# Outputs of the last batch in staging tiles, and a second queue for the last stores

## The chip, the cores and the metric

The kernel runs on one core of one Trainium2 chip. Its time is device microseconds. A run gives one time; the times stated are medians over runs. A profile is taken of one execution and shows every instruction of the engines: TensorE (PE, with its weight loads PEld), VectorE (DVE), ScalarE (ACT), GpSimd (POOL) and SyncE (SP). DMAs are issued from an engine's queue and carried by sixteen DMA engines.

## The reference

Inputs are `q`, `k`, `v` of shape (8, 8, 576, 64), that is batch, head, token, head dimension, and four weights. All are float32.

```
def _attn_ref(q, k, v):
    ...
    out_d = sm_attn(q_d, k_d, v_d)           # attention over means of 4 tokens: 144 x 144
    out_up = np.repeat(out_d, factor, axis=2)
    ...
    mask = np.abs(pos[:, None] - pos[None, :]) < factor
    ...
    out_local = np.matmul(attn, v)           # attention within 3 tokens either way
    return (out_up + out_local).astype(np.float32)

def _moe_ref(x, w_theta, w_tok_r, w_tok_i, w_ch):
    theta = x @ w_theta
    cos_t, sin_t = (np.cos(theta), np.sin(theta))
    zr = x * cos_t
    zi = x * sin_t
    yr = np.einsum('ts,bsd->btd', w_tok_r, zr)
    yi = np.einsum('ts,bsd->btd', w_tok_i, zi)
    y = yr + yi
    u = x + y
    return (u + np.maximum(u @ w_ch, 0.0)).astype(np.float32)
```

The attention's output, with its heads side by side, is `x` of shape (8, 576, 512), and `_moe_ref` of it is the result.

## The kernel before, in words

The work is cut by batch, eight in all. For each batch the attention is computed in blocks, `x` is kept transposed (channels on the partitions) in `xT`, the angles go through sine and cosine on ACT, their products with `x` go into `z`, and the mixing over tokens (`mx`, L636) is the largest part of TensorE's work. Its result plus `x` is `uT`, also transposed.

The last stage, which the change touches, works on `uT` of one batch in chunks of 128 tokens. A batch has 576 tokens: four chunks, numbered 0 to 3, and 64 tokens that are left, the last tokens. These are handled for two batches at a time. Chunk c of batch b is written (b,c) here.

- `du` (L645) transposes `uT` back, token by token, into `ur` with a transposing DMA, one for each 128 channels. It is issued by SP.
- `ch` (L666) is `u @ w_ch` of a chunk, four matmuls into one PSUM bank. For (7,3) it is done in two halves of 256 channels.
- `rl` (L671, in `out_part`) has DVE take the maximum with zero, add `ur`, and write the float32 result to an output tile. `rm` does so for the second half of (7,3).
- `st` (L675, in `out_store`) stores the tile; `su` the second half of (7,3).
- `ut` (L656) copies the last tokens of two batches together, `dt` (L690) transposes them into `utr`, `ht` (L695) is their matmul, `rt` (L699) their result, and `ss` and `sr` (L704) store it, the even batch's 64 partitions and the odd one's.

The output tiles before are five buffers, `osb`, which chunks and last tokens use in turn; a buffer is written again only when its store has landed. Another set, `stg`, holds sixteen slots of 576 float32 on 128 partitions; inputs and some transposes land there. All DMAs of the kernel are issued by SP, whose queue works in order.

The order on every engine is the order of one list of words, `ORDER`, which is written out by hand. A word names a kind of step in its first two letters, and what follows is the PSUM bank, the slot, or the engine. Steps of one kind are taken in the order of batch and chunk. Each instruction is bound behind the one before it on its engine, so that no engine does its instructions in another order. The end of the list, from the matmul for (6,0):

```
ch7 ch6 ss ch5 rl rl ch7 ch6 ch4 ch3 ch2 du du st uta dt rl rl rl rl st
st st st st rl rl st st rm ht7 rt su ss sr k0
```

Here `ch7` is (6,0), the second `ch7` is (6,3), `ch6` (7,0), `ch4` (7,1), `ch3` (7,2) and `ch2` (7,3); the first `st` is (6,0), and the `ss` in the first line belongs to batches 4 and 5.

Of the kernel before, what the change touches and what calls it, by code (L numbers as in the profile page):

```python
# [14 lines left out]
P = 128  # L15
B = 8
# [3 lines left out]
DM = 512  # L20
# [19 lines left out]
HALF = 64  # L40
# [51 lines left out]
nm nd23 xn nd01 st mx6 th7 mx2 cs xn xd3 mx0 ua ua xcv ua ua xt67 utv ct dx st st xt45 xt23 xa ch1 rl th0 ch6 ch1 ch7  # L92
cs xa xa tt0 zz zz th2 th3 cs st du du ch4 rl zz zz ztg ct dz rl mx2 mx0 mx1 cs ua ua st dxe dx ht0 ua th1 cs th3 dx7
dx zz st st mx2 rl mx1 ua ua cs zz dt mx3 mx1 mx2 zz zz ztg dz mx7 ua mx3 du du du mx6 rt ua ua utg ua st rl du st mx7
mx4 ua ua ua sr mx7 mx6 mx5 ua ua ua du du ua ch7 ch6 ss ch5 rl rl ch7 ch6 ch4 ch3 ch2 du du st uta dt rl rl rl rl st
st st st st rl rl st st rm ht7 rt su ss sr k0
"""


# [1 line left out]
def kernel(  # L101
# [11 lines left out]
    nc = tc.nc  # L113
# [4 lines left out]
    def tiles(n, shape, name, dt=BF16):  # L118
        return [pool.tile(list(shape), dt, name=f"{name}{i}") for i in range(n)]
# [35 lines left out]
    rl = tiles(2, [P, 2, 4], "rl", FP32)  # L155
# [13 lines left out]
    NOSB = 5  # L169
    osb = tiles(NOSB, [P, DM], "osb", FP32)  # L170
# [4 lines left out]
    stg = [stga[:, i, :] for i in range(NSTG)]  # L175
# [17 lines left out]
    def constants():  # L193
# [18 lines left out]
        for n, c in enumerate((0, 1, 4)):  # L212
            cuts = []
            lo = [W0[b] - CH * c for b in (2 * c, 2 * c + 1)]
            st = [STEP * b - W0[b] for b in (2 * c, 2 * c + 1)]
            en = [st[g] + OWN[2 * c + g] for g in range(2)]
            dl, ds, de = lo[1] - lo[0] - W, st[1] - st[0], en[1] - en[0]
            cuts = [(lo[0], 1, dl, -4), (3 - lo[0], -1, -dl, 4)]
            if max(st):
                cuts.append((-st[0], 1, -W - ds, 0))  # L220
            if min(en) < W:
                cuts.append((en[0] - 1, -1, W + de, 0))
            select(full[1 + n], KP, cuts)
# [39 lines left out]
    at = {}  # L263
# [394 lines left out]
    def halves(b, c):  # L658

        return [slice(0, DM // 2), slice(DM // 2, DM)] if (b, c) == (B - 1, 3) else [slice(0, DM)]  # L660

    def ch(b, c, w):
        ps = at["ch", b, c] = bank(w)
        for cols in halves(b, c):
            for dc in range(4):
                nc.tensor.matmul(out=ps[:, cols], lhsT=uT[b % 2][:, dc, P * c:P * c + P], rhs=wch[:, dc, cols],  # L666
                                 start=(dc == 0), stop=(dc == 3))

    def out_part(b, c, cols):
        o = osb[(4 * b + c + b // 2) % NOSB]  # L670
        nc.vector.scalar_tensor_tensor(out=o[:, cols], in0=at["ch", b, c][:, cols], scalar=0.0,  # L671
                                       in1=ur[b % 2][:, c, cols], op0=ALU.max, op1=ALU.add)

    def out_store(b, c, cols):
        nc.sync.dma_start(out=out[b, P * c:P * c + P, cols], in_=osb[(4 * b + c + b // 2) % NOSB][:, cols])  # L675

    def rlf(b, c, w):
        out_part(b, c, halves(b, c)[0])

    def rm(b, c, w):  # L680
        out_part(b, c, halves(b, c)[1])

    def st(b, c, w):
        out_store(b, c, halves(b, c)[0])

    def su(b, c, w):
        out_store(b, c, halves(b, c)[1])

    def dt(i, w):
        nc.sync.dma_start_transpose(out=utr, in_=uts[i % 2].rearrange("p e b t -> p (e b t)"))  # L690
# [4 lines left out]
            nc.tensor.matmul(out=ps, lhsT=uts[i % 2][:, dc, :, :], rhs=wch[:, dc, :], start=(dc == 0), stop=(dc == 3))  # L695

    def rt(i, w):
        o = at["ot", i] = osb[(9 * i + 8) % NOSB]
        nc.vector.scalar_tensor_tensor(out=o, in0=at.pop(("ht", i)), scalar=0.0,  # L699
                                       in1=utr.rearrange("p e d -> p (e d)"), op0=ALU.max, op1=ALU.add)  # L700

    def tail_store(e):
        def step(i, w):
            nc.sync.dma_start(out=out[2 * i + e, 512:576, :], in_=at["ot", i][HALF * e:HALF * e + HALF])  # L704
        return step


# [1 line left out]
    def span(*ns):  # L709
        out = [()]  # L710
        for n in ns:
            out = [x + (i,) for x in out for i in range(n)]
        return out

    STEPS = dict(
        k0=(lambda i, w: None, span(1)), kc=(kc, span(4)), la=(la, span(4)), ca=(ca, span(4)), lb=(lb, span(9)), cb=(cb, span(9)), lc=(lc, span(4)), cc=(cc, span(4)),
# [13 lines left out]
        xm=(xm, [(b, c) for b, c in span(B, 4) if b not in XDMA]), dx=(dx, [(b, c) for b, c in span(B, 4) if b in XDMA]), zz=(zz, span(B, 4)), mx=(mx, span(B, 8)),  # L730
        ua=(ua, span(B, 8)), du=(du, [(b, c) for b, c in span(B, 4) if b not in RPE]), ut=(ut, span(B)), ch=(ch, span(B, 4)), rl=(rlf, span(B, 4)),
        st=(st, span(B, 4)), rm=(rm, [(B - 1, 3)]), su=(su, [(B - 1, 3)]), dt=(dt, span(4)), ht=(ht, span(4)), rt=(rt, span(4)), ss=(tail_store(0), span(4)), sr=(tail_store(1), span(4)),
    )

# [68 lines left out]
```

## Time and profile before

| | |
|---|---|
| median of 3 runs | 233.03 us (232.65 to 233.73) |
| the profiled execution | 233.64 us |
| its span, first to last instruction | 231.9 us |
| TensorE busy | 217.4 us, 94% of the span |
| VectorE busy | 189.0 us, 81% |
| ScalarE busy | 154.0 us, 66% |
| GpSimd busy | 148.0 us, 64% |
| moved by DMA | 49.41 MB, 213 GB/s over the span |
| read from and written to HBM | 33.98 MB and 9.44 MB |
| mean granted clock of TensorE | 0.994 |

Times in rows of the profile are microseconds from the start of the span. A row of a timeline gives the start, the length, the engine, the line, the operation, and the tiles (written, read); in brackets the idle time before it on its engine and what ended it. SPq is SP's queue: a row of it is the time in which SP issues a DMA, not the time of the transfer. A landing is when the transfer's last part has arrived. In the page's slices each digit is a fortieth of the span and shows the busy share in tenths.

### The profile page before, as it was taken

Reading aid. Unit: us, or ns where it says so; the run is one execution under the profiler, and the core shown is the slowest. Engines: PE = TensorE matmul, PEld = TensorE weight load, DVE = VectorE, ACT = ScalarE, POOL = GpSimd, SP = SyncE. Lnnn points to the kernel's source line nnn. Section 1 sums busy time; section 2 is a strip of 40 time slices with the busy share of each in tenths; the row PEclk is TensorE's granted clock in tenths of the full one; section 3 lists DMA queues with packets and bytes.
Section 4 is the critical chain, followed back from the end, with each engine's and each line's share of the span. In section 5 each row is a group of like instructions: output and inputs, shape, how many; then the busy total and the mean of one; then the engine's idle time right before and its main releaser. Section 6 shows DMA issues by size and latency. Waiting matters only on the chain. (4 is left out here: it accounts for less than half of the span.)

```text
span 231.9 us, 9404 instructions
## 1 busy us (share of the span) xinstructions
PE 217.4 (94%) x3943; PEld 152.4 (66%) x3970; DVE 189.0 (81%) x370; ACT 154.0 (66%) x240; POOL 148.0 (64%) x194
## 2 busy tenths in 40 slices
PE   7997799999999999999999999989998999999990
PEld 2475677776878666876776685766655765578640
DVE  6599998999988889889989798797986976576462
ACT  2279999479988899898878997778777034230000
POOL 7679999949997997996967689379912010200000
PEclk9999999999999999999999999999999999999997
DMA  6999889999999899999999976980665375565777
GB/s 203 401 391 357 280 185 256 384 271 171 334 306 156 205 280 313 160 206 254 159 273 330 259 128 173 152 162 10 95 159 91 64 195 130 118 176 156 117 218 244
DMA packets 76795, 49.41 MB, mean 213 GB/s; under 512 B 61136, under 2 KB 61392, under 8 KB 76752
## 3 DMA queue, kind: packets, MB, share of 16 engines
q1 hardware_dynamic: 76752, 48.81, 83.9%
q8 instruction: 31, 0.51, 1.0%
q14 instruction: 12, 0.10, 0.2%
HBM read 33.98 MB, written 9.44 MB: 187 GB/s over the span
## 5 line engine op out<-in xcount | busy, mean ns | idle before, releaser
L636 PE MATMUL PS<-WT,z 128*128 128x288 bf16 x576 | 78.2, 286 | 0.3 <-DVE z L615 0.2
L636 PEld LDWEIGHTS <-z 128*128 128x128 bf16 x576 | 53.9, 98 | 16.5 <-issue 1.3
L641 DVE TENSOR_TENSOR uT<-PS,xT 128x288 bf16<-128x288 f32 x64 | 28.5, 452 | 10.3 <-PE PS L636 9.5
L561 ACT ACTIVATE cs<-PS,pihc 128x512 bf16<-128x512 f32 x32 | 22.1, 689 | 21.2 <-PE PS L556 20.8
L556 PE MATMUL PS<-wth,xT 128*128 128x512 bf16 x116 | 30.6, 379 | 0.9 <-DVE xT L545 0.3
L666 PE MATMUL PS<-wch,uT 128*128 128x512 bf16 (+1 forms) x122 | 29.6, 372 | 1.0 <-issue 0.6
L671 DVE SCALAR_TENSOR_TENSOR osb<-PS,ur 128x512 f32<-128x512 f32 (+1 forms) x33 | 21.9, 670 | 8.9 <-DMA ur<-uT 4.3
L524 DVE TENSOR_TENSOR tmp<-PS,rl 128x512 bf16<-128x512 f32 x40 | 27.7, 691 | 1.4
L490 ACT ACTIVATE pm<-PS 128x1024 bf16<-128x1024 f32 (+1 forms) x24 | 20.5, 880 | 6.6 <-PE PS L482 5.5
L545 DVE TENSOR_TENSOR xT<-PS,xdT 128x928 bf16<-128x928 f32 (+1 forms) x24 | 22.3, 952 | 3.2 <-PE PS L482 1.5
L577 POOL TENSOR_TENSOR zT<-xT,cst 128x512 bf16<-128x512 bf16 x7 | 10.2, 1456 | 22.1 <-ACT cst L574 14.1
L295 POOL CAST k_tm<-st 128x576 bf16<-128x576 f32 x23 | 15.9, 704 | 6.4 <-DMA st<-in_k_dram 6.3
L765 ACT ACT_TABLE_LOAD x15 | 19.2, 1283 | 0.3
L666 PEld LDWEIGHTS <-uT 128*128 128x128 bf16 x132 | 11.9, 98 | 11.2
L329 POOL TENSOR_TENSOR two<-qT 128x576 f32<-128x576 bf16 x14 | 16.5, 1176 | 4.4 <-ACT qT L315 4.2
L562 ACT ACTIVATE cs<-PS 128x512 bf16<-128x512 f32 x32 | 19.1, 597 | 0.0
L295 POOL CAST q_tm<-st 128x576 bf16<-128x576 f32 x24 | 16.8, 715 | 2.1 <-DMA st<-in_q_dram 2.0
L556 PEld LDWEIGHTS <-xT 128*128 128x128 bf16 x128 | 11.4, 98 | 10.3 <-DVE xT L545 0.7
L503 POOL TENSOR_TENSOR pm<-pm,band 128x512 bf16<-128x512 bf16 x16 | 18.1, 1151 | 0.0
L396 POOL CAST v_w<-st 128x512 bf16<-128x512 f32 x21 | 13.0, 642 | 7.6 <-DVE osb L671 7.6
L620 DVE TENSOR_TENSOR z<-PS,cs 128x1024 bf16<-128x1024 bf16 x24 | 15.8, 684 | 1.0 <-issue 0.5
L329 POOL TENSOR_TENSOR two<-kT 128x580 f32<-128x580 bf16 x13 | 15.0, 1151 | 1.5 <-ACT kT L315 0.9
(121 smaller groups left out, 419.3 us busy)
## 6 DMA issues: line engine op xcount, KB each, us to landing
st<-in_k_dram SPq DMA_DIRECT2D x32, 288.0 KB, 6.0
st<-in_q_dram SPq DMA_DIRECT2D x32, 288.0 KB, 6.0
st<-in_v_dram SPq DMA_DIRECT2D x70, 128.0 KB, 5.4
out_dram<-osb SPq DMA_DIRECT2D x31, 256.0 KB, 3.6
out_dram<-osb SPq DMA_DIRECT2D x10, 128.0 KB, 2.8
st<-in_v_dram SPq DMA_DIRECT2D x4, 288.0 KB, 3.7
st<-in_moe_w_tok_r_dram SPq DMA_DIRECT2D x4, 288.0 KB, 4.3
st<-in_moe_w_tok_i_dram SPq DMA_DIRECT2D x4, 288.0 KB, 5.8
```

The costliest lines, as they stand in the source:

```text
L295: COPY[w](out=to, in_=of)
L329: nc.gpsimd.tensor_tensor(out=t, in0=src[:, :, 0:2], in1=src[:, :, 2:4], op=ALU.add)
L490: nc.scalar.activation(out=pm[(3 * b + u) % NPM][:, :, 0:n].rearrange("p e c j w -> p e (c j w)"), in_=at.pop(("ps", b, u))[:, :, 0:4 * W ...
L524: nc.vector.tensor_tensor(out=tmp[(NCH * b + c) % NTMP].rearrange("p g (j d) -> p g j d", d=D), in0=ps[:, :, :, 0:D], in1=r.unsqueeze(3).t ...
L545: nc.vector.tensor_tensor(out=xT[b % 2][:, :, lo:lo + cnt].rearrange("p e (m j) -> p e m j", j=4), in0=at.pop(("xt", b, u))[:, :, 0:cnt].r ...
L556: nc.tensor.matmul(out=ps, lhsT=xT[b % 2][:, dc, P * c:P * c + P], rhs=wth[:, dc, :], start=(dc == 0), stop=(dc == 3))
L561: nc.scalar.activation(out=t[:, 0, :], in_=ps, func=AF.Sin, bias=pihc, scale=1.0)
L636: nc.tensor.matmul(out=ps, lhsT=z[b % 2][:, j, P * dc:P * dc + P], rhs=WT[:, j, cols], start=(j == 0), stop=(j == 8))
L641: nc.vector.tensor_tensor(out=uT[b % 2][:, dc, cols], in0=at.pop(("mx", b, i)), in1=xT[b % 2][:, dc, cols], op=ALU.add)
L666: nc.tensor.matmul(out=ps[:, cols], lhsT=uT[b % 2][:, dc, P * c:P * c + P], rhs=wch[:, dc, cols], start=(dc == 0), stop=(dc == 3))
L671: nc.vector.scalar_tensor_tensor(out=o[:, cols], in0=at["ch", b, c][:, cols], scalar=0.0, in1=ur[b % 2][:, c, cols], op0=ALU.max, op1=ALU.add)
L765: nc.scalar.activation(out=idle, in_=pihc, func=TABLE[kind])
```

## The change

Three things change, all at the end of the kernel.

- The four chunks of batch 7 and the last tokens of batches 6 and 7 are written to slots 0 to 3 and 4 of `stg` in place of `osb`.
- Of the last eleven stores, five are issued by ACT's queue (`a` behind the word): (6,1), (6,3), (7,1), the last tokens of batch 6, and the first half of (7,3). The other six stay with SP.
- The last tokens' matmul, result and stores (`ht7`, `rt`, `ss`, `sr`) stand ahead of those of chunk (7,3), which comes last. The stores alternate with the results that they store.

```
-mx4 ua ua ua sr mx7 mx6 mx5 ua ua ua du du ua ch7 ch6 ss ch5 rl rl ch7 ch6 ch4 ch3 ch2 du du st uta dt rl rl rl rl st
-st st st st rl rl st st rm ht7 rt su ss sr k0
+mx4 ua ua ua sr mx7 mx6 mx5 ua ua ua du du ua ch7 ch6 ss ch5 rl rl ch7 ch6 ch4 ch3 du du st uta dt sta rl st rl ht7
+ch2 sta rl st rl sta rl st rt ssa sr rl sta rm su k0
...
+    def obuf(b, c):
+        return stg[c][:, 0:DM] if b == B - 1 else osb[(4 * b + c + b // 2) % NOSB]
+
     def out_part(b, c, cols):
-        o = osb[(4 * b + c + b // 2) % NOSB]
+        o = obuf(b, c)
...
-    def out_store(b, c, cols):
-        nc.sync.dma_start(out=out[b, P * c:P * c + P, cols], in_=osb[(4 * b + c + b // 2) % NOSB][:, cols])
+    QUEUE = dict(a=nc.scalar)
+
+    def out_store(b, c, cols, w):
+        QUEUE.get(w, nc.sync).dma_start(out=out[b, P * c:P * c + P, cols], in_=obuf(b, c)[:, cols])
...
     def st(b, c, w):
-        out_store(b, c, halves(b, c)[0])
+        out_store(b, c, halves(b, c)[0], w)
...
     def su(b, c, w):
-        out_store(b, c, halves(b, c)[1])
+        out_store(b, c, halves(b, c)[1], w)
...
     def rt(i, w):
-        o = at["ot", i] = osb[(9 * i + 8) % NOSB]
+        o = at["ot", i] = stg[4][:, 0:DM] if i == B // 2 - 1 else osb[(9 * i + 8) % NOSB]
...
     def tail_store(e):
         def step(i, w):
-            nc.sync.dma_start(out=out[2 * i + e, 512:576, :], in_=at["ot", i][HALF * e:HALF * e + HALF])
+            QUEUE.get(w, nc.sync).dma_start(out=out[2 * i + e, 512:576, :], in_=at["ot", i][HALF * e:HALF * e + HALF])
         return step
```

## The prediction

> **What bounds it now.** I read the slices of the page first, to see where the kernel stops being a TensorE kernel, then the chain that ended last, then the timelines of the last fifteen microseconds by engine, and last the DMA load in stretches.
>
> ```profile
> span 231.9 us, 9404 instructions
> ...
> PE   7997799999999999999999999989998999999990
> ...
> ACT  2279999479988899898878997778777034230000
> ...
> DMA  6999889999999899999999976980665375565777
> ```
>
> One slice is 5.8 us. TensorE is full up to the last slice and empty in it; ACT is empty in the last four. So all before 218 us is a TensorE matter that the edit does not touch, and the edit lives in the last slices. The profiled execution took 233.64 us beside its span of 231.9 (1.7 us lie around the span) and is 0.61 us above the median of the runs, 233.03. I work out a difference against the span and take it off both.
>
> ```profile
> 218.59 4.06 PE PS L666 x18
> ...
> 222.68 0.59 DVE osb L671
> 223.27 2.29 DMA out_dram<-osb
> ...
> 225.68 0.61 DVE osb L671
> ...
> 226.34 0.77 DVE osb L671 x2
> ...
> 227.11 0.69 DVE osb L699
> ```
>
> That is the end of the chain (start, length, what). The work of TensorE is on it until 222.66; then DVE's last parts wait for a store: a result can be written only when the store that last used its buffer has landed, 2.29 us after it was issued.
>
> ```profile
> 219.22 0.69 DVE L671 SCALAR_TENSOR_TENSOR osb<-PS,ur 128x512 f32<-128x512 f32 x1 [0.41 <-PE PS L666]
> 220.09 0.69 DVE L671 SCALAR_TENSOR_TENSOR osb<-PS,ur 128x512 f32<-128x512 f32 x1 [0.17 <-PE PS L666]
> ...
> 221.82 0.69 DVE L671 SCALAR_TENSOR_TENSOR osb<-PS,ur 128x512 f32<-128x512 f32 x1 [0.17 <-PE PS L666]
> 222.68 0.69 DVE L671 SCALAR_TENSOR_TENSOR osb<-PS,ur 128x512 f32<-128x512 f32 x1 [0.17 <-PE PS L666]
> 223.94 0.69 DVE L671 SCALAR_TENSOR_TENSOR osb<-PS,ur 128x512 f32<-128x512 f32 x1 [0.57 <-DMA out_dram<-osb]
> 225.68 1.41 DVE L671 SCALAR_TENSOR_TENSOR osb<-PS,ur 128x512 f32<-128x512 f32 x3 [1.05 <-DMA out_dram<-osb]
> 227.11 0.69 DVE L699 SCALAR_TENSOR_TENSOR osb<-PS,utr 128x512 f32<-128x512 f32 x1
> ```
> ```profile
> 225.08 1.03 PE L695 MATMUL PS<-wch,ut 128*128 128x512 bf16 x4
> ```
>
> These are chunks (6,0), (6,1), (6,3), (7,0), (7,1), then (7,2) with the two halves of (7,3), then the last tokens. As long as TensorE sets the pace a chunk comes every 0.86 us (219.22 to 220.09) and takes 0.69. Then come the two waits for a landing, 0.57 and 1.05 us. TensorE itself is through at 225.08 + 1.03 = 226.11.
>
> ```profile
> 218.50 2.53 SPq L645 DMA_TRANSPOSE ur<-uT  x2
> 221.46 0.35 SPq L675 DMA_DIRECT2D out_dram<-osb  x1
> 221.93 1.24 SPq L690 DMA_TRANSPOSE utr<-ut  x1
> 223.27 4.70 SPq L675 DMA_DIRECT2D out_dram<-osb  x8
> 228.06 1.14 SPq L704 DMA_DIRECT2D out_dram<-osb  x2
> ```
> ```profile
> 228.62 0.58 SPq L704 DMA_DIRECT2D out_dram<-osb  x1
> ```
>
> SP's queue (the row by itself is the second of the two before it, from a narrower stretch) shows why the landings are late: (6,1) lay ready at 220.78 and was issued at 223.27, behind two transposes for `ur`, the store of (6,0) and the transpose for `utr`. And at the end four stores still stand in line: DVE ends at 227.80, the last store goes out at 228.62, the span ends 3.31 us after that.
>
> ```profile
> 221.00:225.00 4.00, 4.00 (x24) 2.13 (x23) 2.72 (x4) 0.00 (x0) 0.00 (x0) 1.00 0.68 195
> 225.00:230.00 5.00, 1.10 (x7) 0.36 (x4) 2.10 (x4) 0.00 (x0) 0.00 (x0) 0.90 0.97 351
> 230.00:231.00 1.00, 0.00 (x0) 0.00 (x0) 0.00 (x0) 0.00 (x0) 0.00 (x0) 0.50 0.45 98
> ```
> ```profile
> 224.25:229.25 5.00, 1.85 (x13) 1.03 (x11) 2.49 (x5) 0.00 (x0) 0.00 (x0) 0.97 0.97 366
> 229.25:230.50 1.25, 0.00 (x0) 0.00 (x0) 0.00 (x0) 0.00 (x0) 0.00 (x0) 0.50 0.90 211
> ```
>
> These are stretches (from:to, length, busy time of the engines, and in the last two columns the DMA share and GB/s). They hold the second bound: from 225 to 230 the DMA engines are full, with a share of 0.97. In the four microseconds before, they stand idle a third of the time. So an earlier issue gains only what fits into that third.
>
> **The change, part by part.** *Staging tiles* (L671, L699): chunks 0 to 3 of batch 7 and the last tokens of batches 6 and 7 go to `stg` slots 0 to 4 and no longer rotate over the five `osb`. This takes away 0.57 + 1.05 = 1.62 us of waits on DVE. What is late next is TensorE, so most but not all of it is gained. No instruction is added. The slots must be free: the slots' last uses are loads and transposes of earlier stages, and the one slot of 0 to 4 that batch 6 transposed into is read by DVE itself long before. Price nothing.
>
> *Last tokens ahead of the last chunk.* TensorE does the same matmuls and ends at 226.11 as before. `ht` now needs bank 7 from (6,3): read by DVE until 222.51, while TensorE comes to `ht` two matmul groups later, at 223.5 + 0.86 = 224.4. No wait. DVE then goes: (7,0) to 223.37 as before, (7,1) 223.55 to 224.24, (7,2) 224.41 to 225.10, last tokens 225.28 to 225.97, the halves of (7,3) behind the last matmul from 226.13, 0.77 us, to 226.90. Against 227.80 that is 0.90 earlier. (If the first half is released by its own matmuls the end is 226.55; I don't count on it.)
>
> The last tokens also need `utr`, sent by SP at 221.93. Its landing has no row. The nearest is the `ur` transpose of the same size, issued at 219.83 in the same stage, 2.5 us; the far end is the tile's own row from a loaded stage.
>
> ```profile
> ur<-uT SPq DMA_TRANSPOSE x1, 2.5
> ```
> ```profile
> DMA to landing us min/median/max: 4.5/4.5/4.5
> ```
>
> With 2.5 it lands at 224.4, 0.9 before its use, with 4.5 at 226.4. I take 2.5, the same stage; 4.5 becomes a rival. The wait stands in order ahead of both halves of (7,3), so what it costs goes through to the end.
>
> ```profile
> 218.85 0.41 ACT L656 COPY ut<-uT 128x256 bf16<-128x256 bf16 x1 [13.45 <-DVE uT L641]
> ```
> ```profile
> 216.79 1.60 SPq L704 DMA_DIRECT2D out_dram<-osb  x1
> ```
>
> *Five stores on ACT's queue* (`sta`, `ssa`). ACT's last work is the copy to `ut`, done by 219.3 (the first row above), and nothing is behind the stores there, so their waits for DVE hold up nobody. The stores of (6,1), (6,3), (7,1), the even last tokens and the first half of (7,3) go out as DVE ends: 220.8, 222.5, 224.25, 226.0, 226.6. SP keeps (6,0), then past `utr` (6,2) at 223.27, (7,0) at about 223.8, (7,2) at 225.1, the odd last tokens at 226.0 and the last half at 226.92. So the last issue moves from 228.62 to 226.92: 1.70 us earlier, 0.90 by DVE and 0.80 by the queue in which `su` no longer stands behind others, nor others behind it. No row shows an issue by ACT. The bounds are SP's, 0.35 (the row of 221.46) and 1.60 (the row just shown). Five issues in six microseconds have room up to 0.6 each at the tightest place (226.0 to 226.6); I take 0.4 to 0.6, nearest to SP's rows of this stage (eight stores in 4.70 us, waits included, the last store 0.58), and cost it at nothing: TensorE's pace covers it.
>
> ```profile
> out_dram<-osb SPq DMA_DIRECT2D x1, 256.0 KB, 2.4
> ```
>
> *The DMA engines.* Their load from 221 on is the sum of the share column: 4 × 0.68 + 5 × 0.97 + 0.45 = 8.02 us, and it ends at about 230.45. In the changed kernel (6,1) is issued at 220.8. A store of 256 KB takes 2.4 us to land (row above); at the 366 GB/s of the full stretch 0.7 of it is transfer, and of the other 1.7 I put half, 0.9, ahead of the packets (an estimate). So the load is as before up to 221.7, 0.7 × 0.68 = 0.48; the remaining 7.54 at a share of 0.97 take 7.77 us and end at 229.5: a gain of 0.95. The last stretch counts as 0.90 busy but moves 211 GB/s and not 366; these are the two 64-partition stores alone. Its 0.26 MB would take 0.72 us at 366, so 0.53 less when these stores run between others, as they now do. Together 0.95 + 0.53 = 1.48.
>
> By the Trainium skill ("DMA: Bandwidth & Descriptors", section "Issuing engines are not separate DMA queues"), a second issuing engine uses the same 16 DMA engines and saves only the issue time, usually small beside the transfer. By that alone the sum would be the 0.95 of the load; the rows here agree that the engines are full from 225, and add that the issue is not small: 0.35 us for a store and 1.24 for a transpose beside a landing of 2.4.
>
> **Sum.** The issue side allows 1.70, the DMA side 1.48; the later of them decides, and the two queues at the end cost a little: 1.45. Span 231.9 − 1.45 = 230.5; profiled execution 233.64 − 1.45 = 232.2; median 233.03 − 1.45 = 231.6.
>
> **Rivals.** 0.5% is 1.17 us, about what a measurement of this kernel can tell from no change.
>
> *DMA engines bound, without relief.* The 64-partition stores stay slow between the others, and 0.95 is all: 232.1, within 0.5%. For it: the share of 0.97. The page named above would have it so. Against: the stretch from 229.25 is slow only when these stores are alone.
>
> *`utr` late.* Two stores on ACT's queue now run beside that transpose. Landing at 226.4 gives last tokens to 227.1, halves to 227.9, last issue 227.95: a gain of 0.67, 232.4. Against: the `ur` transpose just ahead took 2.5 in a stage with a DMA share of 0.68.
>
> *ACT issues dearly (the other side).* With a price c above 0.6 the first half of (7,3) goes out at 226.0 + c, and the span ends 3.31 + (c − 0.58) later: 226.0 + 2c + 2.73. At c = 1.6, as in the row of 216.79, that is 231.9 of span, no gain; beyond it the change is slower, by 2 us for each us of c: at c = 2.0 by 0.8 us, a median of 233.8. For it: ACT has issued none so far in the program, and transposes do cost SP 1.24. Against: SP's eight stores in a row took 0.59 each, waits included.
>
> *The tiles free nothing.* Were DVE to wait as if the buffers still rotated, (7,1) would start at 223.94 as now; (7,2) would need (6,1), which by ACT's early issue lands at 220.8 + 2.4 = 223.2, so it runs from 224.65 to 225.34, and DVE is back at TensorE's pace with the last tokens: 231.6 to 231.7. So the queue carries the gain, not the tiles; this case needs no chance of its own.
>
> **How the numbers follow.** My sum 0.65, of which a tenth falls within 0.5%; DMA without relief 0.17; `utr` late 0.08; ACT dear 0.07, most of it slower; the rest 0.03. Faster 0.60 (0.58 of the first, 0.02 of the second), within 0.5% 0.32, slower 0.08. The low end is the issue side with the halves released early, 1.70 + 0.35, off the median: 231.0. The high end holds the first three cases and half a spread of the runs (0.5 us): 232.6.
>
> **What would show it.** DVE without a wait for a store behind 222.68, last tokens at 225.3, last half ended by 226.9; ACT's store issues of 0.4 to 0.6 us, the first near 220.8; the DMA share above 0.9 from about 222 instead of 225; the last store issued near 226.9 and the span's end 3.5 us behind it. It is wrong if DVE waits for `utr` (rival two), if ACT's issues exceed 0.6 (rival three), or if the share is full and the last landing 0.5 us later than I say (rival one).

## The result, and the profile after

The changed kernel takes 231.55 us (median of 22 runs) beside 232.89 us for the kernel before (22 runs): ratio 0.9929, 95% interval 0.9901 to 0.9956. That is 1.65 us faster, with an interval of 1.0 to 2.3. Forecast were 231.6 us and 1.45 us. The ratios here and below leave out runs that are more than 1.5% above the fastest of their kernel (7 of the 22 of the changed kernel, 1 of the 22 of the kernel before); over all runs the medians differ by 1.34 us and the means by 0.93.

The page of the changed kernel, with the slices and the DMA queues:

```profile
span 229.3 us, 9430 instructions
...
PE   7997899999999999999999999989998999999992
...
DMA  6999987999998799979799996992473466655787
...
q1 hardware_dynamic: 76096, 47.76, 80.7%
q10 hardware_dynamic: 656, 1.05, 1.3%
```

A second queue, q10, has appeared: ACT's, with the five stores' 1.05 MB. TensorE's last slice is no longer empty. The spans differ by 2.6 us (231.9 and 229.3), which is more than the change can have done: DVE's first result of chunk (6,0) starts at 219.22 before and at 218.04 now, so 1.18 us of the difference lie ahead of anything that was edited. I therefore compare the tail, from that start to the end of the span: 12.7 us before and 11.3 us now, 1.45 less.

DVE's timeline in the tail of the changed kernel (start, length, operation; in brackets its idle time before):

```profile
218.04 0.69 DVE L674 SCALAR_TENSOR_TENSOR osb<-PS,ur 128x512 f32<-128x512 f32 x1 [0.41 <-PE PS L666]
...
221.49 0.69 DVE L674 SCALAR_TENSOR_TENSOR st<-PS,ur 128x512 f32<-128x512 f32 x1 [0.17 <-PE PS L666]
222.42 1.49 DVE L674 SCALAR_TENSOR_TENSOR st<-PS,ur 128x512 f32<-128x512 f32 x2 [0.24 <-PE PS L666]
224.09 0.69 DVE L704 SCALAR_TENSOR_TENSOR st<-PS,utr 128x512 f32<-128x512 f32 x1 [0.18 <-PE PS L700]
224.95 0.76 DVE L674 SCALAR_TENSOR_TENSOR st<-PS,ur 128x256 f32<-128x256 f32 x2 [0.17 <-PE PS L666]
```

Every wait now ends on TensorE; the two that ended on a store, 0.57 and 1.05 us, are gone. DVE ends at 225.71, 7.67 us into the tail (8.58 before).

ACT's queue and SP's queue in the changed kernel:

```profile
219.62 2.06 ACTq L680 DMA_DIRECT2D out_dram<-osb  x2
223.15 0.34 ACTq L680 DMA_DIRECT2D out_dram<-st  x1
224.81 0.55 ACTq L709 DMA_DIRECT2D out_dram<-st  x1
225.46 0.77 ACTq L680 DMA_DIRECT2D out_dram<-st  x1
```
```profile
216.80 2.53 SPq L645 DMA_TRANSPOSE ur<-uT  x2
219.76 0.35 SPq L680 DMA_DIRECT2D out_dram<-osb  x1
220.23 1.31 SPq L695 DMA_TRANSPOSE utr<-ut  x1
221.63 0.53 SPq L680 DMA_DIRECT2D out_dram<-osb  x1
222.26 2.01 SPq L680 DMA_DIRECT2D out_dram<-st  x2
224.81 0.51 SPq L709 DMA_DIRECT2D out_dram<-st  x1
225.74 0.35 SPq L680 DMA_DIRECT2D out_dram<-st  x1
```

The first store on ACT goes out 0.03 us behind DVE's result of (6,1). The last store goes out at 225.74, 7.70 us into the tail (9.40 before), and the span ends 3.56 us behind it (3.31 before).

The DMA load in stretches (the last two columns are the share and GB/s), and the landing of the two halves of (7,3), the first from ACT and the second from SP:

```profile
218.00:221.00 3.00, 3.00 (x15) 1.37 (x14) 2.45 (x4) 0.07 (x1) 0.00 (x0) 1.00 0.63 153
221.00:227.50 6.50, 3.92 (x23) 1.96 (x20) 3.84 (x7) 0.00 (x0) 0.00 (x0) 1.00 1.04 339
```
```profile
out_dram<-st ACTq DMA_DIRECT2D x1, 128.0 KB, 3.0
out_dram<-st SPq DMA_DIRECT2D x1, 128.0 KB, 2.4
```

The engines are full from 3.0 us into the tail; before, it was from 5.8 us. A share above 1 means that transfers overlap in the same engines, each counted with its whole time. The first half, from ACT, lands 3.0 us after the start of its issue, the second, from SP, after 2.4. So ACT's is the later of the two, by some 0.3 us, though it was issued first.

### The profile page after: what moved, and what is told of

The parts are those of the page before. It is cut to its first block, busy times and chain, and to the rows that moved or that the text cites. A ratio compares the mean times of both kernels' runs of the same rounds, so it can differ in the third digit from the quotient of the medians.

```text
span 229.3 us, 9430 instructions
## 1 busy us (share of the span) xinstructions
PE 219.4 (96%) x3970; PEld 152.3 (66%) x3970; DVE 187.8 (82%) x370; ACT 154.3 (67%) x240; POOL 147.4 (64%) x194
## 3 DMA queue, kind: packets, MB, share of 16 engines
q10 hardware_dynamic: 656, 1.05, 1.3%
## 4 chain that ended last, share of the span: by engine, by line
PE 75%; DVE 10%; DMA 5%; POOL 4%; issue 2%; ACT 2%; SPq 0%; DVEq 0%; POOLq 0%; ACTq 0%
PE PS L636 27%; PE PS L666 10%; PE PS L556 10%; PE PS L302 5%; DMA ur<-uT 4%; PE PS L515 2%; PE PS L537 2%; PE PS L595 2%; PE PS L764 2%; PE PS L482 2%; PE PS L568 2%; POOL two L329 1%; POOL pm L503 1%; PE PS L447 1%; DVE pm L505 1%
## 5 line engine op out<-in xcount | busy, mean ns | idle before, releaser
L561 ACT ACTIVATE cs<-PS,pihc 128x512 bf16<-128x512 f32 x32 | 22.1, 690 | 21.0 <-PE PS L556 13.4
L556 PE MATMUL PS<-wth,xT 128*128 128x512 bf16 x128 | 32.1, 379 | 0.1
L666 PE MATMUL PS<-wch,uT 128*128 128x512 bf16 (+1 forms) x132 | 31.1, 373 | 0.0
L674 DVE SCALAR_TENSOR_TENSOR osb<-PS,ur 128x512 f32<-128x512 f32 x28 | 19.1, 685 | 6.7 <-DMA ur<-uT 3.9
L666 PEld LDWEIGHTS <-uT 128*128 128x128 bf16 x132 | 11.9, 98 | 11.2
L396 POOL CAST v_w<-st 128x512 bf16<-128x512 f32 x21 | 13.4, 656 | 8.5 <-DMA st<-in_v_dram 8.5
L556 PEld LDWEIGHTS <-xT 128*128 128x128 bf16 x128 | 11.4, 98 | 10.3 <-DVE xT L545 0.7
```

What stands on the lines that cost most here:

```text
L556: nc.tensor.matmul(out=ps, lhsT=xT[b % 2][:, dc, P * c:P * c + P], rhs=wth[:, dc, :], start=(dc == 0), stop=(dc == 3))
L561: nc.scalar.activation(out=t[:, 0, :], in_=ps, func=AF.Sin, bias=pihc, scale=1.0)
```

## The experiments

Twelve kernels were run. For each, the table has the ratio of its time to the kernel before, the tail of its profiled execution, and how long after the tail's start SP was through with the two last transposes for `ur` (L645). The last column is the tail less that time: what is left once SP is free. The ratios come from the runs, the other columns from one execution each. The changed kernel's ratio is from its own 22 runs; the others come from three later series with 35 runs of the kernel before in each. By the intervals, two ratios can be told apart when they differ by some 0.4 to 0.5%, that is by about 1 us.

| kernel | ratio (95% interval) | tail us | SP free after us | from there to the end us |
|---|---|---|---|---|
| before | 1 | 12.7 | 1.8 | 10.9 |
| changed | 0.9929 (0.9901 to 0.9956) | 11.3 | 1.3 | 10.0 |
| queue alone | 1.0014 (0.9984 to 1.0044) | 11.9 | 0.8 | 11.1 |
| tiles alone | 1.0007 (0.9976 to 1.0038) | 11.7 | 0.8 | 10.9 |
| order alone | 1.0045 (1.0017 to 1.0073) | 13.4 | 1.8 | 11.7 |
| changed, old order | 0.9971 (0.9941 to 1.0000) | 12.3 | 1.9 | 10.3 |
| changed, no tiles | 0.9991 (0.9959 to 1.0023) | 12.2 | 0.8 | 11.4 |
| changed, no ACT queue | 1.0016 (0.9978 to 1.0054) | 12.6 | 1.8 | 10.8 |
| changed, fewer bytes | 0.9933 (0.9904 to 0.9962) | 11.9 | 2.3 | 9.6 |
| changed, stores dealt anew | 0.9928 (0.9889 to 0.9966) | 11.2 | 0.8 | 10.4 |
| before, `dt` on ACT | 0.9993 (0.9953 to 1.0033) | 12.4 | 1.8 | 10.6 |
| changed, last tokens' stores left out | 0.9927 (0.9889 to 0.9965) | 11.7 | 1.7 | 10.0 |
| last tokens ahead of (7,2) | 0.9989 (0.9950 to 1.0027) | 11.2 | 0.9 | 10.3 |
| the same, two banks | 0.9978 (0.9943 to 1.0014) | 11.2 | 0.8 | 10.4 |

The fourth column was not foreseen. SP's time varies by 1.5 us between executions of an order that is the same up to there, and in three of the four kernels with every DMA on SP the tail follows it (10.8 to 10.9 us in the last column); the fourth, the order alone, has new waits.

**The queue alone.** From the kernel before:

```
-rl rl rl rl st st st st st rl rl st st rm ht7 rt su ss sr k0
+rl rl rl rl sta st sta st sta rl rl st sta rm ht7 rt su ssa sr k0
```

> The kernel before with one part of the change: the same five stores go out on ACT's queue; the order is the old one (last tokens last) and all outputs rotate over the five osb buffers. I compare the tail, from the start of DVE's first result of chunk (6,0) to the end of the span: 12.7 us before (231.9 - 219.2), 11.3 us in the changed kernel (229.3 - 218.0). Theory of the queue (early issue fills the idle DMA engines): (6,1) lands near 3.9 us after the tail's start instead of 6.3, so DVE's second wait is gone and the tail is 11.5 to 11.9 us, 0.8 to 1.2 us faster in the median. Rival theory of the tiles (DVE's 1.62 us of waits for a buffer are the gain): the buffers still rotate, so (7,1), the halves of (7,3) and the last tokens wait for landings, the tail stays at 12.3 to 12.7. Rival theory of the order (the 64-partition stores are slow only when they come last and alone): they come last here too, tail 12.2 to 12.5.

No gain, against my theory, though the tail of 11.9 is at the edge of what it gave. DVE's two waits of before are gone, but it found a new one (DVE's timeline and a row of SP's queue):

```profile
225.24 0.76 DVE L674 SCALAR_TENSOR_TENSOR osb<-PS,ur 128x256 f32<-128x256 f32 x2 [1.14 <-DMA out_dram<-osb]
225.91 0.68 DVE L704 SCALAR_TENSOR_TENSOR osb<-PS,utr 128x512 f32<-128x512 f32 x1
```
```profile
221.29 5.07 SPq L680 DMA_DIRECT2D out_dram<-osb  x4
```

The halves of (7,3) need the buffer of (6,2), whose store SP issued at 221.29, and it landed just ahead of 225.24, 3.8 us later. With the stores on their way earlier, each takes longer to land. The rotation that had been covered is not covered any more.

**The tiles alone.** The buffers as changed, the old order, all stores on SP (no `a` in the list).

> The kernel before with one part of the change: the outputs of batch 7 and its last tokens in staging slots; old order, all stores on SP. Theory of the queue: DVE loses its two waits and ends 0.9 us earlier, but SP issues the second store as late as before (behind the transpose for utr), the DMA engines fill at the same time and carry the same bytes, so the tail is 12.4 to 12.7 us and the median within 0.3 us of before. Theory of the tiles: the last issue on SP follows DVE, tail 11.6 to 11.9, 0.8 to 1.1 us faster. Theory of the order: 12.4 to 12.7 as well.

The median is unchanged, as the theory of the queue had it. The tail is 11.7, as the theory of the tiles had it, and not 12.4 to 12.7. The reason lies in SP's rows:

```profile
226.32 0.69 DVE L704 SCALAR_TENSOR_TENSOR st<-PS,utr 128x512 f32<-128x512 f32 x1
```
```profile
216.89 3.33 SPq L645 DMA_TRANSPOSE ur<-uT  x2
...
227.24 1.15 SPq L709 DMA_DIRECT2D out_dram<-st  x2
```

DVE starts its last result at 226.32, but SP issues the last two stores only from 227.24 on. In this execution SP was free at 220.22, 0.8 us into the tail; before, at 221.03, 1.8 us into it. From there to the end it is 10.9 us in both kernels, with DVE's waits and without them. So I read it that before the change SP's queue set the end, and that DVE's 1.62 us cost next to nothing.

**The order alone.** The new list without `a`, buffers rotating.

> The kernel before with one part of the change: the last tokens' matmul, result and stores ahead of chunk (7,3), stores alternating with results; all stores on SP, buffers rotate. Theory of the queue: DVE's waits for (6,0), (6,1) and now also for (6,3) and (6,2) ahead of the last tokens and of (7,3) remain, so that (7,3) ends later than before and the tail is 12.4 to 13.0 us, no gain or a little worse. Theory of the tiles: 12.5 to 13.0. Theory of the order: the 64-partition stores run between others, tail 12.1 to 12.3, about 0.5 us faster.

Slower by 0.45%, and the tail of 13.4 is beyond what any theory gave. DVE waits three times for a store:

```profile
223.15 0.69 DVE L674 SCALAR_TENSOR_TENSOR osb<-PS,ur 128x512 f32<-128x512 f32 x1 [0.76 <-DMA out_dram<-osb]
224.71 0.69 DVE L674 SCALAR_TENSOR_TENSOR osb<-PS,ur 128x512 f32<-128x512 f32 x1 [0.87 <-DMA out_dram<-osb]
226.12 0.69 DVE L704 SCALAR_TENSOR_TENSOR osb<-PS,utr 128x512 f32<-128x512 f32 x1 [0.72 <-DMA out_dram<-osb]
```

The third is new: the last tokens come one result earlier and need the buffer of (6,3). What stands behind them on DVE, the halves of (7,3), is late with them.

**The change with the old order.** Tiles and queue, the list of the first experiment.

> The changed kernel with one part undone: the last tokens come last again, as before; staging slots and ACT's five stores stay. My sum had 0.53 us for the 64-partition stores that no longer run alone at the end. If that term is right, the tail is 11.7 to 11.9 us here against 11.3. If the term is nothing and the issue side alone decides: DVE ends at the same time, the last two stores are issued side by side right behind it, tail 11.1 to 11.4.

Part of the gain seems lost (0.9971), at the edge of what the runs can tell from the changed kernel, and not by the mechanism that I expected.

```profile
227.04 0.69 DVE L704 SCALAR_TENSOR_TENSOR st<-PS,utr 128x512 f32<-128x512 f32 x1 [1.03 <-DMA utr<-ut]
```

DVE is through with the chunks and waits 1.03 us for `utr`, issued by SP at 222.05, almost 5 us earlier. This is my second rival, in this kernel. The 64-partition stores are not told apart by it.

**The change without the tiles.** The new list with ACT's five stores, buffers rotating.

> The changed kernel with one part undone: the outputs rotate over the five osb buffers again; ACT's five stores and the new order stay. New theory (the parts are limits in series, each alone only uncovers the next): in the new order the buffers' stores are issued long before they are needed again. With the landings of the changed kernel's profile, (7,1) would wait for (6,0) until 4.95 us after the tail's start (0.55 late), the last tokens for (6,3) until 6.15 and the halves for (6,2) until 6.7, which is when they come anyway; DVE ends 0.1 us later, tail 11.2 to 11.6 us against 11.3, the median 0.5 to 0.7% below before. Theory of the tiles (the waits for buffers are the gain): the waits return, tail above 12, no gain against before.

The gain is gone: 0.9991. My new theory had expected 11.2 to 11.6 and fails in its numbers; the theory of the tiles is nearer. DVE's timeline, and the landing of (6,2) and (6,3), in this order, from SP and ACT:

```profile
226.88 0.69 DVE L704 SCALAR_TENSOR_TENSOR osb<-PS,utr 128x512 f32<-128x512 f32 x1 [1.00 <-PE PS L666]
227.49 0.74 DVE L674 SCALAR_TENSOR_TENSOR osb<-PS,ur 128x256 f32<-128x256 f32 x2
```
```profile
out_dram<-osb SPq DMA_DIRECT2D x1, 256.0 KB, 3.8
out_dram<-osb ACTq DMA_DIRECT2D x1, 256.0 KB, 3.4
```
```profile
out_dram<-osb ACTq DMA_DIRECT2D x1, 256.0 KB, 3.5
utr<-ut SPq DMA_TRANSPOSE x1, 3.9
```

The idle 1.00 us is put down to TensorE, which by then had long gone on; the last tokens' buffer is that of (6,3), which landed at 226.7. The second fence is of the stretch just before: (6,1) on ACT took 3.5 us to land and `utr` 3.9. I had reckoned with 2.4 and 2.5.

**The change without ACT's queue.** The new list without `a`, staging tiles.

> The changed kernel with one part undone: all stores on SP; staging slots and the new order stay. Theory of limits in series: SP's issue, behind the two transposes, starts the stores 1 us or more later and the DMA engines fill as late as in the kernel before; the order saves up to 0.5 us. Tail 11.5 to 12.2, median 0 to 0.3% below before. If the queue gave nothing (tiles and order carry the gain): tail 11.2 to 11.4, the whole 0.7%.

The gain is gone here too: 1.0016. DVE and SP:

```profile
226.11 0.75 DVE L674 SCALAR_TENSOR_TENSOR st<-PS,ur 128x256 f32<-128x256 f32 x2 [0.18 <-PE PS L666]
```
```profile
218.46 2.53 SPq L645 DMA_TRANSPOSE ur<-uT  x2
...
226.65 1.27 SPq L709 DMA_DIRECT2D out_dram<-st  x2
228.01 1.05 SPq L680 DMA_DIRECT2D out_dram<-st  x2
```

DVE ends at 226.86, 7.67 us into the tail, exactly as in the changed kernel; the order and the tiles are those of the changed kernel. But SP, which has eleven stores and `utr` to issue one behind the other, is still at the last tokens when DVE is done, and the last store goes out 9.46 us into the tail and not 7.70. The Trainium skill ("DMA: Bandwidth & Descriptors", section "Issuing engines are not separate DMA queues") has a second issuing engine save only the issue time, usually small beside the DMA. The traces agree that the engines are shared, with a share of 1.04 over 6.5 us; the issue time is not small here: the last store goes out 1.76 us later with one queue, 0.5 of which is that SP was free later in this execution (1.8 us into the tail, and 1.3 in the changed kernel's).

**Fewer bytes.** Of six stores only 128 columns:

```
     def out_store(b, c, cols, w):
+        if (b, c) in ((6, 1), (6, 2), (6, 3), (7, 0), (7, 1), (7, 2)):
+            cols = slice(0, DM // 4)
```

> The changed kernel with less to store: of (6,1), (6,2), (6,3), (7,0), (7,1), (7,2) only 128 of 512 columns are stored; every issue, wait and order stays. That leaves out 1.2 MB, some 2.9 us of full DMA engines. If the DMA engines set the end, the transposing DMA for the last tokens lands in 2.6 us instead of 3.8, the last stores land in 2.3 to 2.5 us instead of up to 3.0, and the tail falls from 11.3 to 10.6 to 10.9 us, where the last issue and its landing set it. If the issue side sets the end already, the tail stays at 11.2 to 11.4.

The ratio, 0.9933, is that of the changed kernel with all bytes (0.9929), but it can't tell the two theories apart: 0.4 to 0.7 us is less than the runs resolve. The tail doesn't either. In this execution SP was free only 2.3 us into it, and the first three results of batch 7 wait 1.11 us; the row names TensorE, which keeps its pace, so that `ur`, whose last transpose went out late, is what is left:

```profile
222.44 1.89 DVE L674 SCALAR_TENSOR_TENSOR st<-PS,ur 128x512 f32<-128x512 f32 x3 [1.11 <-PE PS L666]
```

What decides is the stretch in which the last stores go out, and the landing of the two halves of (7,3):

```profile
225.50:226.50 1.00, 0.00 (x0) 0.00 (x0) 0.47 (x2) 0.00 (x0) 0.00 (x0) 1.00 0.00 1
```
```profile
out_dram<-st ACTq DMA_DIRECT2D x1, 128.0 KB, 3.1
out_dram<-st SPq DMA_DIRECT2D x1, 128.0 KB, 2.8
```

The DMA engines stand empty for a whole microsecond (a share of 0.00), and still the halves take 3.1 and 2.8 us to land, no less than the 3.0 and 2.4 of the changed kernel. From the last issue to the end it is 3.9 us. So the bytes of the middle stores do not set the end.

**The stores dealt anew.** 

```
-ch7 ch6 ch4 ch3 du du st uta dt sta rl st rl ht7
-ch2 sta rl st rl sta rl st rt ssa sr rl sta rm su k0
+ch7 ch6 ch4 ch3 du du uta dt sta sta rl sta rl st ht7
+ch2 rl sta rl st rl sta rt ssa sr rl sta rm su k0
```

> The changed kernel with stores dealt out anew: ACT takes (6,0), (6,1), (6,2), (7,0), (7,2), the even last tokens and the first half of (7,3); SP issues the transpose for the last tokens right behind those for ur and then (6,3), (7,1), the odd last tokens and the last half. The first store goes out 1.0 us earlier and the last tokens' transpose 0.8 us earlier. If the DMA engines set the end, their work begins up to 0.7 us earlier and the tail is 10.7 to 11.1 us against 11.3, the median 0.8 to 1.0% below before. If the last issue and its landing set it, 11.2 to 11.4, as the changed kernel.

DVE, SP's last store and ACT's first stores:

```profile
224.91 0.76 DVE L674 SCALAR_TENSOR_TENSOR st<-PS,ur 128x256 f32<-128x256 f32 x2 [0.18 <-PE PS L666]
```
```profile
225.69 0.34 SPq L680 DMA_DIRECT2D out_dram<-st  x1
```
```profile
218.72 2.06 ACTq L680 DMA_DIRECT2D out_dram<-osb  x3
```

The first store goes out 0.72 us into the tail and not 1.58, and the end is where it was: 11.2, and 0.9928. DVE ends at 7.67 and the last store goes out at 7.69. The ratio can't tell 0.7 from 0.8 to 1.0%, but in the trace the last issue decides once more, not when the engines begin.

**`dt` on ACT.** The kernel before with one instruction moved.

```
-        nc.sync.dma_start_transpose(out=utr, in_=uts[i % 2]...
+        (nc.scalar if w == 'a' else nc.sync).dma_start_transpose(out=utr, in_=uts[i % 2]...
```

> The kernel before with one instruction moved: the transpose for the last tokens (dt) is issued by ACT and not by SP, nothing else. In the kernels that keep all stores on SP the tail so far followed the time at which SP got to its last ur transpose: the last store went out 8.8 us after that in all three (8.79, 8.77, 8.87). Theory of SP's queue (SP, not DVE's waits, sets the end before): without the 1.24 us of dt the stores from (6,1) on go out 1.3 us earlier and the last store goes out 7.8 to 8.1 us after the last ur transpose, where DVE sets it; the tail, counted from that transpose, falls from 12.1 to 11.1 to 11.4 us, the median 0.3 to 0.5% below before. Theory of DVE's waits alone: they shrink too (the landings come earlier), but as taking them away whole gave nothing, no gain here either: 12.0 to 12.2. If ACT's transpose has to wait for SP's to land and then delays the last tokens, 11.5 to 12.

The last expectation came (11.8 us, counted as there), and so the run doesn't decide on SP's queue. ACT's transpose goes out late:

```profile
221.52 1.54 ACTq L690 DMA_TRANSPOSE utr<-ut  x1
```
```profile
225.82 0.69 DVE L699 SCALAR_TENSOR_TENSOR osb<-PS,utr 128x512 f32<-128x512 f32 x1 [0.53 <-DMA utr<-ut]
```

ACT had copied its source by 218.2, but issues it at 221.52, 3.4 us into the tail (2.7 before, on SP) and 0.3 us after SP's last transpose has landed. The trace names no releaser; that it waits for this landing is inferred. It lands 4.2 us later, and DVE waits for it. Of the 1.24 us that SP saved, 0.3 are left: the last store goes out 9.1 us into the tail (9.4 before).

**The last tokens' stores left out, and two further versions.** The first leaves `ss` and `sr` of batches 6 and 7 out. The other two have the list

```
+ch7 ch6 uta ch4 ht0 ch3 du du dt sta sta rl sta rl st
+ch2 rl sta rl st rt ssa sr rl st rl sta rm su k0
```

and the last of them `ch25` for `ch2`, with the second half of (7,3) in bank 5.

> The changed kernel without the two 64-partition stores of the last tokens of batches 6 and 7 (they are left out). In the changed kernel the last four stores land at 9.2, 9.7, 10.1 and 10.4 us of the tail, one behind the other. If these four queue on the DMA engines, the two halves of (7,3) land 2.3 to 2.4 us after their issue here, at 9.8 and 10.1, and the tail is 10.9 to 11.0 us. If the landing of the first half, 3.0 us, is a matter of ACT's queue alone (its issue took 0.77 us), the tail stays at 11.2 to 11.3.

> A version that takes up what the runs showed: as the run with the stores dealt out anew, and the last tokens' matmul and result one chunk earlier still, ahead of (7,2), so that their slow 64-partition stores are under way when the halves of (7,3) are ready. DVE ends as before that (7.7 us of the tail, TensorE sets it). If the last four stores queue on the DMA engines, the last landing comes at 10.0 to 10.2 instead of 10.4 and the tail is 10.8 to 11.0 us. If the transpose for the last tokens lands later than 5.2 us of the tail (it landed at 5.0), DVE waits and the tail is 11.2 or more.

> The version before this one, and the second half of (7,3) in a PSUM bank of its own, so that DVE can begin the first half while TensorE still works on the second. DVE ends 0.1 us earlier than 7.7 (its own five results from 5.2 on fill the time) if it is then the bound; tail 10.7 to 10.9 us; the median 0.9 to 1.1% below before. If the second bank brings nothing, the tail is that of the version before this one.

Without the two stores the ratio is 0.9927, as with them, which again can't tell a few tenths of a microsecond. Its trace, of an execution of 234.05 us whose tail begins at 220.7, shows two things (DVE's wait for the last tokens, and the landing of the two halves, from ACT and SP):

```profile
228.28 0.69 DVE L704 SCALAR_TENSOR_TENSOR st<-PS,utr 128x512 f32<-128x512 f32 x1 [1.74 <-DMA utr<-ut]
```
```profile
out_dram<-st ACTq DMA_DIRECT2D x1, 128.0 KB, 1.7
```
```profile
out_dram<-st SPq DMA_DIRECT2D x1, 128.0 KB, 1.8
```

SP got to `utr` 2.6 us into the tail here (2.2 in the changed kernel's execution); it landed 4.9 us later, and DVE waited 1.74 us for it, which makes the tail 11.7. And the halves land 1.7 and 1.8 us after their issue, where they took 3.0 and 2.4 behind the two 64-partition stores; ACT's issue is back from 0.77 to 0.34 us. In the run of the queue alone, where the halves go out ahead of these stores, they also land in 1.7 and 1.8 us. So in the changed kernel the two stores lengthen the way to the end: from the last issue it is 3.56 us there and 2.7 here.

The two further versions reach the tail of 11.2, no better than the changed kernel, and their ratios, 0.9989 and 0.9978, are not better either. The second bank lets DVE end 0.27 us earlier, at 227.25, 7.40 us into the tail (the three last results together):

```profile
225.90 1.35 DVE L676 SCALAR_TENSOR_TENSOR st<-PS,ur 128x512 f32<-128x512 f32 x3 [0.17 <-PE PS L668]
```

It gains nothing: 11.2. The last tokens' stores, (7,2) and the two halves are issued within 1.5 us there, and the end is 3.8 us behind the last issue in place of 3.56. Why their ratios are 0.5 to 0.6% above that of the changed kernel, little more than the runs can tell apart, stays open; their tails begin at 219.5 and 219.9, where the changed kernel's begins at 218.0, so that the difference would lie ahead of the tail. No version faster than the changed kernel was found.

## Why the prediction was right, and where its working was not

- *DVE's path* came out to a hundredth: forecast end 226.90 − 219.22 = 7.68 us into the tail, measured 7.67. TensorE is what is late next, and the halves do wait for the last matmul. There was luck in it, which the point on `utr` tells.
- *The last issue* came out as well: 226.92 − 219.22 = 7.70, measured 7.70.
- *ACT's issues* cost 0.34 to 0.55 us, and one 0.77, which is above the 0.4 to 0.6 that I took and, by my own sign, speaks for the third rival. It came in small: the store with the 0.77, the first half of (7,3), lands last, about 0.3 us behind SP's. Without the 64-partition store ahead of it, it was issued in 0.34.
- *From the last issue to the end* I had 3.31 and a little, 3.56 in all; measured 3.56. The little is ACT's: its last store lands 3.0 us after the start of its issue.
- *The DMA engines* were a step that failed. They fill as early as forecast, but that does not set the end: it came no sooner when the engines stood empty ahead of the last stores, nor with a first store 0.86 us earlier. The term of 0.53 us for the 64-partition stores was not seen. From the last issue to the end it is 3.31 us with these stores last and 3.56 with them ahead of the halves, and the halves land in 3.0 and 2.4 us behind them, in 1.7 and 1.8 without them. The issue side alone gives 9.40 − 7.70 = 1.70 us, less 0.25 for the longer landing: 1.45. So the sum had the right figure with a wrong second line.
- *`utr`* was mis-sized: 3.9 us to land beside ACT's stores (row of the kernel without tiles), up to 4.9 in other runs, not 2.5; the 4.5 that I made a rival was nearer. In the changed kernel it cost nothing: DVE took it up at 224.09, at most 3.86 us after its issue. That was luck. I had it issued 2.71 us into the tail, and in the execution that was profiled SP came to it at 2.19. Issued at 2.6, in the run without the last tokens' stores, it held DVE for 1.74 us; in the old order, issued at 2.9, for 1.03. The second rival is thus a matter of when SP is free, and my 0.08 for it looks low.
- *"The tiles free nothing"* was wrong, and I had given it no chance. Without the tiles the gain is gone (0.9991), since landings take 3.4 to 3.8 us there, with two queues feeding the engines, and not 2.4. Nor does "the queue carry the gain": alone it gives 1.0014.
- *What set the end before* I had not said plainly. I listed DVE's waits and SP's queue side by side, and one reading was wrong: when DVE ends, at 227.80, not four stores stand in line but two, with a third being issued. The runs fit that SP's queue set it (10.8 to 10.9 us from SP free to the end, with tiles or without), and that DVE's waits lay beside it. The one run meant to decide it, `dt` on ACT, did not. Nor is it told apart from the DMA engines, which were full from 5.8 us into the tail: SP's issues may have been paced by them, and no run took bytes from the kernel before. What is shown is that the queue and the tiles are both needed, as without either the gain is gone; for the order the loss is at the edge of the noise. In the traces the parts are limits in series: SP's queue, then the rotating buffers, then the last tokens behind `utr`. Taking one away uncovers the next, so no part alone is faster, and the three together are.
- *The size* of 1.45 us owes something to the execution that was profiled. There SP was free 1.8 us into the tail. With SP free at 0.8, as in five other executions, the same rule of 10.9 us gives the kernel before a tail of 11.7, and the change would gain 0.45. The 22 runs say 1.65 with an interval of 1.0 to 2.3, and 1.34 or 0.93 by the medians or means of all. So that the forecast met the size is in part luck.

## What to carry to other kernels

When several limits end within a microsecond of each other, a part of a change tested by itself can show nothing and still be needed; undo each part in turn as well. Compare the stretch that was edited, from a common event to the end, and not the spans. A landing time measured with one queue did not hold once a second queue fed the same engines: price buffers and transposes with the longer one.

## What the runs showed that I had not expected

- The transposing DMA for `utr` landed in 2.6 us with every DMA on SP and in 3.7 to 4.9 us beside the other queue's stores. A plain 256 KB store of the tail took 2.3 to 3.0 us with one queue and up to 4.7 with two.
- SP is held for 0.1 to 1.5 us at one place shortly ahead of the tail, in every execution, but at a different instruction: a store's issue of 1.60 us in the kernel before (0.51 usual), a pair of `ur` transposes of 3.33 us in the tiles' run (2.53 usual). An instruction fetch falls into the same microseconds each time; whether it is the cause was not tried.
- The start of the tail varies from 218.0 to 220.7 us between kernels that are the same up to there. This is more than the change gains, and it is why it takes 22 runs to see it.
